# Sliding-window attention and a gated feed-forward block: sums ahead of numerators, masks moved to another engine, and two value steps moved

## The chip, the cores and the metric

The kernel runs on one core of a Trainium2 chip. The metric is the device time of one execution in microseconds (us), as the median of several runs. The engines are PE (TensorE, matmuls), DVE (VectorE), ACT (ScalarE), POOL (GpSimd) and SP, which issues transfers. Each engine works through its own list of instructions in order; semaphores make one wait for another.

## The reference

```python
def _attn_ref(q, k, v):                  # each (8, 8, 576, 64): batch, head, position, width
    scores = scale * np.matmul(q, k.transpose(0, 1, 3, 2))
    rel = pos[:, None] - pos[None, :]
    mask_plain = (rel >= 0) & (rel < 32)
    mask_dil = (rel >= 0) & (rel < 128) & (rel % 4 == 0)
    masks = mask_plain for heads 0 to 3, mask_dil for heads 4 to 7
    scores = np.where(masks, scores, -1e9)
    attn = np.exp(scores - max)
    attn = attn / (sum(attn) + 1e-09)
    return np.matmul(attn, v)

def _moe_ref(x, w_gate, w_val, w_out):   # x: (4608, 512)
    g = x @ w_gate                       # 512 x 1536
    gelu = 0.5 * g * (1.0 + erf(g / sqrt(2)))
    return (gelu * (x @ w_val)) @ w_out  # 1536 x 512
```

The attention's output, with heads side by side, is the x of the second part. Inputs and outputs are fp32; the kernel works in fp16 with fp32 sums.

## The kernel before, in words

**Units.** Attention is done in 32 units n = 0 to 31, each two heads of one batch: batch n // 4, with n % 4 = 0, 1 plain (window of 32) and n % 4 = 2, 3 dilated (every fourth position). A unit goes through four steps, each with its helper:

- Scores: `emit_s` multiplies keys by queries within the band (12 or 10 narrow matmuls, L339 or L369) into four banks of PSUM, and ACT takes the exponential (L349 and L350, or L371) into a tile `P` in SBUF.
- Mask, in one of two ways. With `pe_mask` four matmuls of an identity by a bias tile (L332, L355) put a large negative number into the banks ahead of the scores, and the exponential gives zeros. Without it, `emit_s` hands back a function `emit_mask`, which multiplies `P` by a 0/1 mask on DVE (L379). The set `biased` (L683) names the units that get their mask on PE.
- Values: `emit_pv` multiplies `P` by the values (numerators, "num") and by a tile of ones (sums of weights, "den"), all matmuls at L442. In the narrow form, used in output stages, both lie in three neighbouring banks, V to V+2: the numerators of a plain unit in columns 0 to 575 and its sums in 960 to 1535; those of a dilated unit in 0 to 287 and 512 to 799, and its sums in the rest of the three banks. In the wide form the sums of a dilated unit have two banks of their own.
- Normalisation on DVE: `norm_r` turns the sums over with a 32x32 transpose (dt, L500), takes the reciprocal (rc, L505) and turns it back (rb, L507); `norm_x` multiplies the numerators by it into `xT` (L518 plain, L521 dilated), the x of the feed-forward part.

**Chunks.** The feed-forward part runs over nine chunks c of 512 tokens. Its first half, `ffn1` (L533; `ffn1_two`, L545, for the first two blocks where x comes late), makes 12 blocks of `u_all`, with a GELU on ACT (L557) and a product on DVE (L558) for each. Its second half, here called output stage c, is `ffn2` (L564): four token blocks tb of twelve 512-wide matmuls each, with a copy out of PSUM on ACT (L575) and a store at the end of each.

**Order.** The order of every engine is the order in which the program is written (a manual schedule). Attention units are put between the matmuls of the output stages at places written out by hand: `places` holds for each stage a list such as `1.5s 1.9v`: in token block 1, ahead of matmul 5, the scores of the next unit of `scores[c]`; ahead of matmul 9 the values of the next unit of `values_b[c]`. A 12 means after the block. Output stages 1 and 2 share the list `four`: stage 1 has the scores of units 9, 10 and 11 and the values of 8, 9, 10 and 11 (batch 2), stage 2 the scores of 13, 14, 15 and 16 and the values of 12 to 15 (batch 3). The scores of units 8 and 12 come at the end of the `ffn1` before. A "v" runs the function `pv` of the stage:

```python
def pv(last):
    n = todo.pop(0)
    emit_pv(n, V)
    if not last:
        mask_next()
    norm(n, V)
```

`mask_next` emits the next pending `emit_mask`, if that unit has one. In stages 1 and 2 it stands for the unit whose scores came last. After the stage, `ffn1_two` of the next chunk needs the `xT` of the stage's four units, one for each quarter of its matmuls; the last unit fills the last quarter.

Batches 3 and later are loaded during earlier chunks: loads by SP, casts to fp16 on POOL (L199, L200 for queries and keys, L183, L187 for values).

Of the kernel before, what the change touches and what calls it, by code (L numbers as in the profile page):

```python
# [38 lines left out]
def kernel(  # L39
# [11 lines left out]
    B, H, S, D = q.shape  # L51
    NT, DM = out.shape
    DFF = moe_w_gate.shape[1]
    P = 128
# [11 lines left out]
    PW, PT, DW = 160, 64, 2 * NCL  # L66
    PB = 3 * PW
    PH = PB + P + PT
# [18 lines left out]
    ones = const.tile([P, CH], F16, tag="ones")  # L87
# [165 lines left out]
    def is_plain(n):  # L253
        return n % NHP < NHP // 2
# [125 lines left out]

        return emit_mask

    def emit_pv(n, b0, parts=("num", "den"), wide=False):


        b, hp = n // NHP, n % 2
        vp, vd, vt, vr = tiles["v", b]
        pt = tiles["P", n]
        mms = []

        def add(hl, c0, dims, lhs, p0, pdims, st):

            base = ps[64 * hl : 64 * hl + 64, b0 + c0 // 512, c0 % 512 : c0 % 512 + 1]
            o = bass.AP(tensor=base.tensor, offset=base.offset, ap=[base.ap[0]] + dims)
            rhs = bass.AP(tensor=pt.tensor, offset=pt.offset + p0, ap=[pt.ap[0]] + pdims)
            mms.append((o, lhs, rhs, st))

        def run(n):
            return [[1, n]]

        if is_plain(n):
            if "num" in parts:
                for j in range(5):
                    for hl in range(2):
                        lhs = vp[:, j, hp, 2 * hl, :] if j < 4 else vt[:, hp, 2 * hl, :]
                        w = (PW, PW, PW, P, PT)[j]
                        add(hl, j * P, run(w), lhs, hl * PH + j * PW - (32 if j == 4 else 0), run(w), j in (0, 4))
            if "den" in parts:
                d0 = 1024 if wide else 960

                groups = (
                    ((0, 0, 4, P), (P, P, 3, 32), (PH - PT, 512, 1, PT))
                    if wide
                    else ((0, 0, 1, 64), (64, 64, 1, 64), (PW, P, 3, P), (P, P, 3, 32), (PH - PT, 512, 1, PT))
                )
                for i, (p0, q0, runs, w) in enumerate(groups):
                    for hl in range(2):
                        st = i == 0 or i == (2 if wide else 1)
                        add(hl, d0 + q0, [[P, runs], [1, w]], ones[:, 0:D], hl * PH + p0, [[PW, runs], [1, w]], st)
        else:  # L420
            if "num" in parts:
                for s in range(2):
                    for m in range(3):
                        for hl in range(2):
                            h, p0 = 2 * hp + hl, (2 * s + hl) * DW
                            if m < 2:
                                add(hl, 512 * s + m * NCL, run(P), vd[:, h, 2 * m + s, :], p0 + m * NCL, run(P), m == 0)
                            else:
                                two = [[NCL, 2], [1, 16]]
                                add(hl, 512 * s + P, two, vr[:, h, s, :], p0 + P, two, False)  # L430
            if "den" in parts:

                groups = (
                    ((0, 0, DW, 1024), (1, 0, DW, 1536))
                    if wide
                    else ((0, 0, 192, 288), (0, 192, 96, 800), (1, 0, 96, 896), (1, 96, 192, 1312))
                )
                for i, (s, c, w, c0) in enumerate(groups):
                    for hl in range(2):
                        add(hl, c0, run(w), ones[:, 0:D], (2 * s + hl) * DW + c, run(w), wide or i != 2)  # L440
        for o, lhs, rhs, st in mms:
            nc.tensor.matmul(o, lhs, rhs, start=st, stop=True, skip_group_check=True)  # L442

# [184 lines left out]
    def den(n, b0, wide=False):  # L628
        emit_pv(n, b0, ("den",), wide)
        norm_r(n, b0, wide)  # L630

    def num(n, b0):
        emit_pv(n, b0, ("num",))
        norm_x(n, b0)
# [45 lines left out]
    scores = {0: range(4, 8), 1: range(8, 12), 2: range(12, 17), 3: range(17, 22), 4: range(22, 27), 5: range(27, 32)}  # L680
    values_b = {1: range(8, 12), 2: range(12, 16), 3: range(17, 20), 4: range(22, 24), 5: range(27, 28)}
    values_a = {3: {4: 16}, 4: {2: 20, 6: 21}, 5: {1: 24, 4: 25, 7: 26}, 6: {1: 28, 4: 29, 7: 30, 10: 31}}
    biased = (6, 7, 8, 9, 10, 11, 12, 13, 14, 15)  # L683

    four = "1.5s 1.9v 1.12s 2.6v 2.12s 3.3v 3.12s 3.12v"
    three = "1.4s 1.12v 2.3s 2.12v 3.2s 3.12s 3.12v"
    two = "1.4s 1.12v 2.3s 2.12v 3.2s 3.12s"
    one = "1.4s 1.12v 2.3s 2.12s 3.6s"
# [3 lines left out]
    for c in range(NCH):  # L692
# [11 lines left out]
        for nb in range(NNB):  # L704
            if nb == 0 and c < 2:
                ffn1_two(c, (4, 6) if c == 0 else (6, 0))
            elif nb == 0 and late == "x":
                ffn1_two(c, pairs)
            elif nb > 1 or c > 2 and late != "x":
                ffn1(c, nb, pairs[(nb + swap) % 2])  # L710
            if pend is not None:
                (norm_both_x if is_plain(pend) else norm_x)(pend, SB)
                pend = None
            if nb in pv_at:
                pend = pv_at[nb]
                if is_plain(pend):
                    emit_both(pend, SB)
                    norm_both_r(pend, SB)
                else:
                    emit_pv(pend, SB, wide=True)  # L720
                    norm_r(pend, SB, wide=True)
            if c == 0 and nb in (9, 10):
                t_plain(1, q61, nb - 9, 4 + 2 * (nb - 9), ("act", "dve"))
            if c == 0 and nb in (8, 11):
                rr = rd1.rearrange("p t h r d -> p t (h r d)")
                hp = nb // 11
                t_dil(1, hp, qd1, 4096 + 512 * hp, 5120 + 512 * hp, ("dve", "dve"))
                t_rest(1, hp, (rr[:, 0], rr[:, 1]), 6144 + P * hp)
            if nb == NNB - 1 and c > 0 and s_list:
                n = s_list.pop(0)  # L730
                masks.append(emit_s(n, SB, pe_mask=n in biased))
# [106 lines left out]
```

The softmax here doesn't subtract the row's maximum and nothing guards it: scores larger than these inputs give would overflow.

## Time and profile before

| | |
|---|---|
| median of 7 runs | 362.05 us (360.91 to 363.0) |
| the profiled execution | 362.21 us, of which the span is 360.1 us |
| granted PE clock | 0.991 of full |
| L564, one 512-wide matmul of output stages, x432 | 380 ns from start to end |
| L500 and L507, transposes on DVE | 780 and 778 ns |
| L505, reciprocal | 267 ns |
| L518 and L521, normalised product, plain and dilated | 751 and 1124 ns |
| L371, exponential of a dilated unit | 1129 ns |
| L349 and L350, exponential of a plain unit | 970 and 488 ns |
| L575, copy out on ACT | 597 ns |
| output stage 1, and start of `ffn1_two` behind it | 90.5 to 108.2 us |
| output stage 2, and start of `ffn1_two` behind it | 130.8 to 148.5 us |

One execution was profiled, and all times of single instructions come from it. Matmuls overlap one another, so the time from one start to the next is less than the duration of one. In rows of groups and of the timeline stand the start, the duration, engine, line, operation, the tile written and the tiles read, and in brackets the idle time of the engine before it and whose end it waited for. A row of the waits names the waiting engine and line, the one waited for, the total in us, the number of waits and the longest.

### The profile page before, as it was taken

To read this page: it belongs to the slowest core of one execution; us is meant where nothing else is said; L and a number is where in the kernel's file an instruction comes from. 1 tells how busy PE (TensorE), PEld (TensorE's weight loads), DVE (VectorE), ACT (ScalarE), POOL (GpSimd) and SP (SyncE) were. 2 spreads that over 40 slices of the span, in tenths; PEclk is the share of its full clock that TensorE was granted. 3 is DMA by queue.
4 is the path that set the end of the run, shared out by engine and by line. 5 is a ranking of instruction groups with operands and counts; after the bars stand their busy time and mean duration, and the time that the engine had idled before them with its cause. 6 is when DMAs were issued, how large, how long until landed. Compare 5 with 4: busy or idle time off the path is not lost.

```text
span 360.1 us, 5997 instructions
## 1 busy us (share of the span) xinstructions
PE 344.2 (96%) x2358; PEld 165.7 (46%) x2358; DVE 196.2 (54%) x298; ACT 145.9 (41%) x212; POOL 78.3 (22%) x110
## 2 busy tenths in 40 slices
PE   6789899999989999899999999999999999999995
PEld 2554354444544445444444444544454444444442
DVE  3585446744266325765479838893679613403320
ACT  2633255254542354433653355436543223312321
POOL 2580334540531540054003420050000000000000
PEclk9969999999999999999999999999999999999999
DMA  8999999999899896599438962794100020011002
GB/s 207 233 177 214 215 156 197 191 155 247 185 120 233 185 147 128 140 183 136 102 102 175 156 104 85 170 154 91 60 29 0 19 99 2 1 64 54 0 29 87
DMA packets 107291, 45.30 MB, mean 126 GB/s; under 512 B 83040, under 2 KB 102496, under 8 KB 107264
## 3 DMA queue, kind: packets, MB, share of 16 engines
q1 hardware_dynamic: 84272, 31.21, 38.7%
q0 software_dynamic: 21456, 12.01, 27.5%
q10 hardware_dynamic: 1536, 1.70, 2.0%
q8 instruction: 18, 0.29, 0.4%
q14 instruction: 9, 0.07, 0.1%
HBM read 40.13 MB, written 9.44 MB: 138 GB/s over the span
## 4 chain that ended last, share of the span: by engine, by line
PE 82%; DMA 10%; DVE 4%; POOL 1%; ACT 1%; issue 0%; SPq 0%; POOLq 0%; ACTq 0%
PE ps L533 44%; PE ps L564 26%; DMA qd<-in_k_dram 5%; PE ps L442 4%; DMA xT<-in_q_dram 3%; PE ps L545 3%; DMA vr<-in_v_dram 2%; PE ps L339 1%; DVE xT L521 1%; PE ps L369 1%; PE ps L455 1%; DVE dt L500 1%; DVE rb L507 1%; PE ps L355 1%; PE ps L332 1%; DVE P L379 0%
## 5 line engine op out<-in xcount | busy, mean ns | idle before, releaser
L557 ACT ACTIVATE g<-ps 128x512 f16<-128x512 f32 x108 | 63.6, 597 | 124.3 <-PE ps L533 110.9
L558 DVE SCALAR_TENSOR_TENSOR u_all<-g,ps 128x512 f16<-128x512 f16 x108 | 72.6, 683 | 75.4 <-PE ps L533 66.2
L564 PE MATMUL ps<-wo,u_all 128*128 128x512 f16 x432 | 101.0, 380 | 0.4 <-ACT osb L575 0.3
L533 PE MATMUL ps<-xT,wg 128*128 128x512 f16 x392 | 100.7, 379 | 0.2
L533 PE MATMUL ps<-xT,wv 128*128 128x512 f16 x392 | 100.6, 379 | 0.0
L564 PEld LDWEIGHTS <-u_all 128*128 128x128 f16 x432 | 39.2, 98 | 44.6 <-issue 0.5
L533 PEld LDWEIGHTS <-wv 128*128 128x128 f16 x392 | 38.3, 98 | 46.5 <-issue 0.2
L533 PEld LDWEIGHTS <-wg 128*128 128x128 f16 x392 | 37.2, 98 | 44.7 <-issue 2.0
L575 ACT ACTIVATE osb<-ps 128x512 f32<-128x512 f32 x33 | 19.7, 597 | 48.4 <-PE ps L564 48.4
L500 DVE STREAM_TRANSPOSE dt<-ps 128x576 f32<-128x576 f32 x25 | 19.5, 780 | 25.2 <-PE ps L442 25.1
L199 POOL CAST qp<-st 128x2048 f16<-128x2048 f32 x6 | 11.4, 1893 | 100.6 <-DMA st<-in_k_dram 51.1
L507 DVE STREAM_TRANSPOSE rb<-rc 128x576 f32<-128x576 f32 x32 | 24.9, 778 | 1.1
L371 ACT ACTIVATE P<-ps 128x1152 f16<-128x1152 f32 x16 | 18.1, 1129 | 12.7 <-PE ps L369 12.7
L349 ACT ACTIVATE P<-ps 128x960 f16<-128x960 f32 x16 | 15.5, 970 | 9.4 <-PE ps L339 9.3
L521 DVE TENSOR_TENSOR xT<-ps,rb 128x576 f16<-128x576 f32 x16 | 17.8, 1124 | 0.3
L577 DVE TENSOR_SCALAR osb<-ps 128x512 f32<-128x512 f32 x3 | 2.1, 692 | 27.8 <-PE ps L564 27.8
L545 PE MATMUL ps<-xT,wg 128*128 128x512 f16 x40 | 15.4, 385 | 1.4 <-DVE xT L521 0.9
L545 PE MATMUL ps<-xT,wv 128*128 128x512 f16 x40 | 15.2, 380 | 0.0
L442 PE MATMUL ps<-P,ones 128*64 128x192 f16 (+5 forms) x174 | 11.6, 248 | 1.6 <-DVE P L379 0.7
L379 DVE TENSOR_TENSOR P<-P,mask_p 128x1344 f16<-128x1344 f16 x10 | 9.2, 926 | 6.8 <-ACT P L350 6.8
L379 DVE TENSOR_TENSOR P<-P,mask_d 128x1152 f16<-128x1152 f16 x8 | 6.1, 757 | 11.1 <-ACT P L371 11.1
L470 DVE STREAM_TRANSPOSE dt<-ps 64x576 f32<-64x576 f32 x14 | 10.9, 780 | 0.4
(83 smaller groups left out, 268.0 us busy)
## 6 DMA issues: line engine op xcount, KB each, us to landing
out_dram<-osb SPq DMA_DIRECT2D x36, 256.0 KB, 2.0
sv<-in_v_dram SPq DMA_DIRECT2D x40, 128.0 KB, 3.7
st<-in_q_dram SPq DMA_DIRECT2D x24, 128.0 KB, 3.5
st<-in_k_dram SPq DMA_DIRECT2D x24, 128.0 KB, 2.9
qd<-in_q_dram POOLq DMA_DIRECT2D x7, 256.0 KB, 4.9
qd<-in_k_dram POOLq DMA_DIRECT2D x7, 256.0 KB, 6.9
vd<-in_v_dram POOLq DMA_DIRECT2D x7, 256.0 KB, 6.9
wg<-in_moe_w_gate_dram POOLq DMA_DIRECT2D x3, 512.0 KB, 8.2
```

The costliest lines, as they stand in the source:

```text
L349: nc.scalar.activation(pt[:, :, 0:PB], sb[:, 0, :, 0:PB], AF.Exp, bias=0.0, scale=scale)
L371: nc.scalar.activation(pt, ps[:, b0 : b0 + 4, 0:DW], AF.Exp, bias=0.0, scale=scale)
L442: nc.tensor.matmul(o, lhs, rhs, start=st, stop=True, skip_group_check=True)
L500: nc.vector.transpose(dst, den)
L507: nc.vector.transpose(rb.rearrange("p (b c) -> p b c", c=32), bass.AP(tensor=rc.tensor, offset=rc.offset, ap=[rc.ap[0], [1, 18], [0, 32]]),)
L521: nc.vector.tensor_tensor(dst.rearrange("p (i m s) -> p i m s", m=2, s=2), num, rb.rearrange("p (s m i) -> p i m s", s=2, m=2), ALU.mult,)
L533: nc.tensor.matmul(ps[:, b0 + gi, :], w[:, kc, ns], xT[kc][:, tok], start=(kc == 0), stop=(kc == NKC - 1))
L545: nc.tensor.matmul(ps[:, pairs[nb] + gi, :], w[:, kc, ns], xT[kc][:, tok], start=(kc == 0), stop=(kc == NKC - 1),)
L557: nc.scalar.activation(g, ps[:, b0, :], AF.Gelu)
L558: nc.vector.scalar_tensor_tensor(u_all[:, nb, :], g, USCALE, ps[:, b0 + 1, :], ALU.mult, ALU.mult)
L564: nc.tensor.matmul(ps[:, bank, :], u_all[:, fc, tb * P : (tb + 1) * P], wo_t[fc // 4][:, fc % 4, :], start=(fc == 0), stop=(fc == NNB - 1),)
L575: nc.scalar.activation(osb, ps[:, bank, :], AF.Copy, bias=0.0, scale=1.0 / USCALE)
```

## The change

Three edits. `emit_pv` emits the sums of weights before the numerators, in both forms. The units 9, 10, 11, 13, 14 and 15 leave the set `biased`, so that their masks are multiplied on DVE; 6, 7, 8 and 12 stay. In the list `four`, the first values go from 1.9 to 1.6 and the second from 2.6 to 2.4.

```diff
-    def emit_pv(n, b0, parts=("num", "den"), wide=False):
+    def emit_pv(n, b0, parts=("den", "num"), wide=False):
...
         if is_plain(n):
-            if "num" in parts:
-                for j in range(5):
-                    ...
             if "den" in parts:
                 d0 = 1024 if wide else 960
...
                         add(hl, d0 + q0, [[P, runs], [1, w]], ones[:, 0:D], hl * PH + p0, [[PW, runs], [1, w]], st)
+            if "num" in parts:
+                for j in range(5):
+                    ...
         else:
+            if "den" in parts:
+                groups = (...)
+                ...
             if "num" in parts:
                 for s in range(2):
...
-            if "den" in parts:
-                groups = (...)
-                ...
         for o, lhs, rhs, st in mms:
             nc.tensor.matmul(o, lhs, rhs, start=st, stop=True, skip_group_check=True)
...
-    biased = (6, 7, 8, 9, 10, 11, 12, 13, 14, 15)
+    biased = (6, 7, 8, 12)
 
-    four = "1.5s 1.9v 1.12s 2.6v 2.12s 3.3v 3.12s 3.12v"
+    four = "1.5s 1.6v 1.12s 2.4v 2.12s 3.3v 3.12s 3.12v"
```

The loops that move (shown as `...`) are the same before and after.

More of the change, by code (lines that the diff above doesn't have):

```diff
@@ L401, in emit_pv @@
         if is_plain(n):
-            if "num" in parts:
-                for j in range(5):
[L404 to L407, printed above, removed]
             if "den" in parts:
@@ L419, in emit_pv @@
                         add(hl, d0 + q0, [[P, runs], [1, w]], ones[:, 0:D], hl * PH + p0, [[PW, runs], [1, w]], st)
-        else:
+            if "num" in parts:
+                for j in range(5):
+                    for hl in range(2):
+                        lhs = vp[:, j, hp, 2 * hl, :] if j < 4 else vt[:, hp, 2 * hl, :]
+                        w = (PW, PW, PW, P, PT)[j]
+                        add(hl, j * P, run(w), lhs, hl * PH + j * PW - (32 if j == 4 else 0), run(w), j in (0, 4))
+        else:
+            if "den" in parts:
+                groups = (
+                    ((0, 0, DW, 1024), (1, 0, DW, 1536))
+                    if wide
+                    else ((0, 0, 192, 288), (0, 192, 96, 800), (1, 0, 96, 896), (1, 96, 192, 1312))
+                )
+                for i, (s, c, w, c0) in enumerate(groups):
+                    for hl in range(2):
+                        add(hl, c0, run(w), ones[:, 0:D], (2 * s + hl) * DW + c, run(w), wide or i != 2)
             if "num" in parts:
@@ L430, in emit_pv @@
                                 add(hl, 512 * s + P, two, vr[:, h, s, :], p0 + P, two, False)
-            if "den" in parts:
[L433 to L440, printed above, removed]
         for o, lhs, rhs, st in mms:
```

## The prediction

> **What bounds the kernel now.** I read the page first, then the waits of PE, then the chain of waits through output stages 1 and 2, then the timeline of DVE, ACT and POOL around them. A unit is a pair of heads (32 units, four to a batch). "pv" of a unit is its 20 matmuls of L442: numerators, and sums of weights against ones.
>
> ```profile
> PE 344.2 (96%) x2358; PEld 165.7 (46%) x2358; DVE 196.2 (54%) x298; ACT 145.9 (41%) x212; POOL 78.3 (22%) x110
> ```
>
> PE is busy for 96% of the span, so whatever PE no longer does looks like a gain, and DVE at 54% looks free. But these are averages. The waits of PE show where it isn't the bound:
>
> ```profile
> PE ps L442 <- DVE xT L521: 1.8, 2, 1.1
> ...
> PE ps L545 <- DVE xT L521: 0.9, 2, 0.5
> ```
>
> Four waits, 2.7 us, and all four are at the end of output stages 1 and 2, the two stages that the change edits. There PE waits for DVE's normalisation (L521). The chain of waits through stage 2:
>
> ```profile
> 134.66 0.57 PE ps L332 x4
> ...
> 138.06 0.49 PE ps L355 x4
> ...
> 142.44 0.49 PE ps L355 x4
> 142.93 0.37 PE ps L369 x12
> 143.30 0.75 PE ps L564 x3
> 144.06 0.68 PE ps L442 x20
> 144.75 0.80 DVE dt L500
> 145.57 0.28 DVE rc L505
> 145.88 0.79 DVE rb L507
> 146.69 1.14 DVE xT L521
> 147.83 0.04 issue
> 147.87 0.74 PE ps L442 x16
> 148.64 0.80 DVE dt L500
> ```
>
> L332 and L355 are bias masks on PE: they are what is removed. From 144.75 on the chain is DVE: the normalisation of unit 14 (dt, rc, rb, xT: 3.07 us), pv of unit 15, its normalisation, and only then the last quarter of L545, at 151.75. So the stage ends at a fixed distance, 7.0 us, behind the start of dt for its third unit, if DVE does nothing else in between. Stage 1 is alike: dt of unit 10 at 104.44, L545 freed at 111.42. **What counts is when that third dt starts**; the sum below is made on it.
>
> **Part 1, the bias masks.** Units 9, 10, 11 (stage 1) and 13, 14, 15 (stage 2) lose four matmuls each: by the rows 0.57 us for 9 and 13, 0.49 for the other four, 3.10 us of PE in all. In their place each gets a multiply of its weights on DVE (L379). The prices:
>
> ```profile
> 54.44 0.86 DVE L379 TENSOR_TENSOR P<-P,mask_p 128x1344 f16<-128x1344 f16 x1 [2.43 <-ACT P L350]
> 58.55 1.57 DVE L379 TENSOR_TENSOR P<-P,mask_p 128x1344 f16<-128x1344 f16 x1
> 176.35 0.76 DVE L379 TENSOR_TENSOR P<-P,mask_d 128x1152 f16<-128x1152 f16 x1 [2.21 <-ACT P L371]
> ```
>
> 0.86 plain, 0.76 dilated. The 1.57 lay over two POOL casts (58.37 to 60.37). The place matters more than the price: `pv` emits a unit's matmuls, then the multiply of the next unit, then the normalisation. So dt now queues on DVE behind a multiply that waits for ACT's exponential of the next unit. Behind dt stand the rest of the normalisation and, through it, the next pv on PE, which needs the banks.
>
> **Part 2, values sooner.** The first pv goes from behind nine matmuls of the second token block to behind six, one matmul after the scores of the next unit; the second from behind six matmuls of the third block to behind four. The second to third scores thus move behind 8 matmuls after the second pv instead of 6. Values loads are no issue: those of batch 2 were cast by 72.6, used at 96.2; those of batch 3 by 99.6, used at 136.5. No DMA is moved.
>
> **Part 3, sums ahead of numerators.** The matmuls are the same and so I cost PE at nothing. A gain would need dt to start before the numerators end. In the narrow form used in output stages, sums and numerators share banks (plain: bank V+1; dilated: V and V+1). In the trace one row shows how such a case waits: two groups of transposes go to the first bank, columns 0 to 127 and 128 to 255, and the second waited for the copy of the first, which ended at 16.75.
>
> ```profile
> 16.80 0.66 PE L312 MATMUL ps<-ident,xT 16*128 16x16 f32 x8 [0.95 <-DVE qTd L315]
> ```
>
> So a wait goes by bank and not by column. dt then waits for the last numerator, just as it waited for the last sum: 0 us. Only the wide dilated form keeps them in separate banks (units 26, 30, 31); dt comes some 0.3 us sooner there, in stages where PE waits for nothing: 0 us as well.
> The Trainium skill, "PSUM — Partial Sum Buffer", section "PSUM bank collisions raise a hardware error", says to guard by bank, not by address, which speaks against this part in the same way; by that rule the sum is the one below, by columns it would be the first rival's.
>
> **The sum, stage 2.** A 512-wide matmul takes 0.216 us (17 from 130.81 to 134.49), a turn to narrow ones 0.10. Scores of 13 start at 134.49 + 0.10 = 134.59. From scores to the end of the exponential a plain unit took 1.85 us (54.84 to 56.69): 136.44. Multiply: +0.03 + 0.86 = 137.33. dt of unit 12 at 137.36; before it was 137.35. So the normalisation of 12 ends where it did (2.79 us: 140.15), and pv 13 starts at 140.20 against 140.26. PE is there long before: scores 0.40, one matmul 0.32, pv 0.72, six 1.40, scores 0.37, four 0.96 make 138.76. It waits 1.4 us, a new wait that eats the bias time saved on 13 and 14.
> Then pv 13 to 140.91; eight matmuls to 142.64; ACT stores the block 0.20 behind (142.84 to 143.44; before it began at 142.48), and only then does the exponential of 15: 143.44 + 1.13 = 144.57 (its scores, at 142.74, would have allowed 143.22). Multiply +0.03 + 0.76 = 145.36. dt of 14 at 145.39 instead of 144.75: **+0.64 us**. With the old places, 6 matmuls instead of 8 there, it would be 0.43 less.
> **Stage 1** is the same to a few hundredths, but POOL casts until 96.28 and the multiply of 9 would be ready at 96.16. By the 1.57 row, where the multiply ended 0.7 after the first cast did, it waits: +0.12. dt of 8 is at 97.17 (97.10 before), dt of 10 at 105.15 (104.44): **+0.71 us**. Bounds of this meeting: nothing, or the whole of the two casts that run there, 2.45 us, if the data they wait for land 2.4 us later.
> The Trainium skill, "SBUF — State Buffer", section "Who interferes with whom", has such a multiply, of two SBUF inputs, block wholly against a POOL read that came first; that would make the same +0.12.
>
> Behind the third dt nothing changes, so the sum is **+1.35 us**: 362.21 of the profiled run (span 360.1 and 2.1 around it) to 363.6, and on the median of 362.05, 363.4. The saved 3.10 us of PE shows up as PE's idle time. A difference under 0.3% (1.1 us) is about what can't be told from none.
>
> **The rivals.**
> Faster: dt waits by columns. Then the sums of 13 are done while its numerators wait for unit 12; after that wait only 0.30 us of PE remain instead of 0.71, so dt of 14 comes at 140.50 + 1.73 + 0.20 + 0.60 + 1.13 + 0.03 + 0.76 + 0.03 = 144.98, late by 0.23, but dt of 15 follows the product of 14 at once instead of 0.82 later (147.82 to 148.64). Net -0.57 a stage, -1.1 to -1.35 for both as the turns fall: 360.8. Against it stands the row at 16.80. For it: no row shows DVE reading a bank beside PE's writing.
> About the same: the multiply of the third unit is ready sooner, if ACT does the exponential of 15 ahead of the store or PE's wait before pv 13 is shorter than 1.4. With the multiply fully hidden, dt of 14 follows pv 14, at 144.65: -0.1 a stage, 361.85. Against it: ACT's order is the program's, and the store comes first.
> Slower by more: the multiply of 9 in stage 1 meets the 1.89 us cast of L199. That cast waits for a load, from 80.2 to 93.83; should it start later than 94.4, it holds the multiply for what is left of it, and the whole chain of stage 1 moves with it: up to 1.9 to 2.4 us, 365.3 to 365.8.
>
> **How the numbers follow.** My sum 0.70 (in four fifths of it over 1.1 us: 0.56 slower, 0.14 same), waits by column 0.10 (faster), multiply hidden 0.10 (0.08 same, 0.02 faster), meeting the cast 0.10 (slower). That makes faster 0.12, same 0.22, slower 0.66. My sum's own terms (1.85 of the exponential, 0.10 of a turn, the meeting on POOL) reach from about 362.4 to 364.8. The range goes from 361.2 (leaving out the first rival) to 365.0 (leaving out most of the last).
>
> **What would show it.** Right: L442 waits for L518 in both stages, some 1.4 us each, and for L521 some 1.9 and 1.5 us (1.1 and 0.7 before); dt of the third unit ends its idle time with the multiply of L379 just before it; L545 is freed 0.6 to 0.7 later from the stage's start. Wrong: dt of L500 beginning within the numerators of its own unit in these stages; no wait of L442 at the second pv; or PE's idle time growing by less than 3 us, which would mean that a part of the bias time came through as a gain.

## The result and the profile after

The changed kernel takes 363.69 us (median of 13 runs, 362.66 to 364.56), the kernel before 362.06 us (32 runs): a ratio of 1.0047, 95% interval 1.0036 to 1.0058, or 1.6 us slower. The forecast was 363.4. The profiled execution took 363.28 us with a span of 361.2, against 362.21 and 360.1.

First the page of the changed kernel, the busy time of each engine:

```profile
PE 341.7 (95%) x2334; PEld 165.6 (46%) x2334; DVE 200.4 (55%) x304; ACT 145.4 (40%) x212; POOL 78.1 (22%) x110
```

PE does 2.5 us less than before (344.2), in a span 1.1 us longer: its idle time grew from 15.9 to 19.5 us. On balance all of that lies in stages 1 and 2: from the first L564 of the stage to the last quarter of L545 PE is idle for 6.3 us in the two together, against 2.7 before. Where it went stands in the waits of PE (total, number, longest):

```profile
PE ps L442 <- DVE xT L521: 2.2, 2, 1.3
...
PE ps L442 <- DVE xT L518: 1.9, 2, 1.1
PE ps L564 <- ACT osb L575: 1.6, 5, 0.3
...
PE ps L545 <- DVE xT L521: 1.0, 2, 0.5
...
PE ps L442 <- DVE xT L480: 0.3, 1, 0.3
```

New are the waits for L518, one in each of the stages 1 and 2 at the second pv (1.06 and 0.85 us), and the one for L480, which lies in chunk 5 and not in these stages at all. L564's waits for the copy of L575 rise from 0.3 us to 1.6: the four new ones, 0.31 us each, lie in the two stages too. They don't add to the stage's length, since two of them come ahead of PE's longer wait for L518 in the same stage and the other two while the chain below runs through ACT and DVE. The chain of waits through stage 2 has turned from PE to DVE and ACT:

```profile
136.33 0.49 ACT P L350
136.82 0.02 issue
136.84 0.86 DVE P L379
137.70 0.70 DVE dt L500
...
139.61 0.77 DVE xT L518
140.38 0.04 issue
140.42 0.78 PE ps L442 x20
141.21 1.85 PE ps L564 x8
143.05 0.02 issue
143.08 0.40 ACT osb L575
143.48 0.09 issue
143.57 1.13 ACT P L371
144.70 0.02 issue
144.73 0.76 DVE P L379
145.49 0.70 DVE dt L500
...
152.40 0.81 PE ps L545 x3
```

The reader sees the sum of the prediction link by link: exponential, multiply (L379), normalisation, the second pv, eight matmuls, the store's copy, the exponential of unit 15, its multiply, and the third dt. (In this view a piece begins where the one before it ends; by the timeline, which the table below uses, that dt starts at 145.40.) The distance from the start of the stage's first token block to the third dt is the number to watch, because from there to the last quarter of L545 both kernels need 7.0 us:

| third dt, us after the stage's start | stage 1 | stage 2 |
|---|---|---|
| before | 104.44 - 90.50 = 13.94 | 144.75 - 130.81 = 13.94 |
| changed | 104.81 - 90.39 = 14.42 | 145.40 - 131.18 = 14.22 |

That is +0.48 and +0.28 us. A third piece lies behind the stages: from the wait of L545 for L349 in chunk 4 to the end of the span the kernel before takes 360.1 - 186.38 = 173.72 us, the changed one 361.2 - 187.03 = 174.17, +0.45. The three make 1.21 us; the start-up was 0.11 shorter in this run. It differs from run to run: up to the start of stage 1 all kernels of this document run the same program, and in their ten profiled runs that point lies between 89.82 and 91.61 us.

### The profile page after: what moved, and what is told of

Same layout as the page of the kernel before. It is cut to its first block, busy times and chain, and to the rows that moved or that the text cites. A ratio compares the mean times of both kernels' runs of the same rounds, so it can differ in the third digit from the quotient of the medians.

```text
span 361.2 us, 5953 instructions
## 1 busy us (share of the span) xinstructions
PE 341.7 (95%) x2334; PEld 165.6 (46%) x2334; DVE 200.4 (55%) x304; ACT 145.4 (40%) x212; POOL 78.1 (22%) x110
## 4 chain that ended last, share of the span: by engine, by line
PE 78%; DVE 11%; ACT 4%; DMA 3%; issue 2%; ACTq 0%; DVEq 0%
PE ps L533 42%; PE ps L564 24%; PE ps L545 4%; DMA xT<-in_k_dram 3%; PE ps L442 3%; DVE rb L507 2%; DVE dt L500 2%; PE ps L339 1%; DVE P L379 1%; DVE dt L470 1%; DVE xT L521 1%; ACT P L371 1%; ACT osb L575 1%; PE ps L369 1%; DVE u_all L558 1%
## 5 line engine op out<-in xcount | busy, mean ns | idle before, releaser
L558 DVE SCALAR_TENSOR_TENSOR u_all<-g,ps 128x512 f16<-128x512 f16 x108 | 72.6, 683 | 76.2 <-PE ps L533 65.1
L564 PE MATMUL ps<-wo,u_all 128*128 128x512 f16 x432 | 100.9, 380 | 1.7 <-ACT osb L575 1.6
L533 PE MATMUL ps<-xT,wg 128*128 128x512 f16 x392 | 100.7, 379 | 0.2
L533 PE MATMUL ps<-xT,wv 128*128 128x512 f16 x392 | 100.6, 379 | 0.0
L564 PEld LDWEIGHTS <-u_all 128*128 128x128 f16 x432 | 39.7, 98 | 45.8 <-issue 1.7
L533 PEld LDWEIGHTS <-wv 128*128 128x128 f16 x392 | 38.3, 98 | 46.4 <-issue 0.3
L533 PEld LDWEIGHTS <-wg 128*128 128x128 f16 x392 | 37.3, 98 | 44.1 <-issue 1.4
L575 ACT ACTIVATE osb<-ps 128x512 f32<-128x512 f32 x33 | 19.7, 597 | 51.5 <-PE ps L564 51.5
L379 DVE TENSOR_TENSOR P<-P,mask_p 128x1344 f16<-128x1344 f16 x12 | 10.9, 915 | 18.4 <-ACT P L350 18.4
L349 ACT ACTIVATE P<-ps 128x960 f16<-128x960 f32 x16 | 15.5, 970 | 8.3 <-PE ps L339 8.2
L521 DVE TENSOR_TENSOR xT<-ps,rb 128x576 f16<-128x576 f32 x16 | 17.8, 1125 | 0.3
L442 PE MATMUL ps<-P,ones 128*64 128x192 f16 (+5 forms) x174 | 11.9, 251 | 6.3 <-DVE xT L521 2.2
L545 PE MATMUL ps<-xT,wg 128*128 128x512 f16 x40 | 15.8, 396 | 1.5 <-DVE xT L521 1.0
L379 DVE TENSOR_TENSOR P<-P,mask_d 128x1152 f16<-128x1152 f16 x12 | 9.1, 756 | 12.3 <-ACT P L371 12.3
L545 PE MATMUL ps<-xT,wv 128*128 128x512 f16 x40 | 15.7, 392 | 0.0
L442 PEld LDWEIGHTS <-ones 128*64 128x64 f16 x174 | 7.3, 111 | 14.7 <-issue 13.4
```

Source lines behind the costliest of these rows:

```text
L379: nc.vector.tensor_tensor(pt, pt, mb, ALU.mult)
L521: nc.vector.tensor_tensor(dst.rearrange("p (i m s) -> p i m s", m=2, s=2), num, rb.rearrange("p (s m i) -> p i m s", s=2, m=2), ALU.mult,)
L533: nc.tensor.matmul(ps[:, b0 + gi, :], w[:, kc, ns], xT[kc][:, tok], start=(kc == 0), stop=(kc == NKC - 1))
L545: nc.tensor.matmul(ps[:, pairs[nb] + gi, :], w[:, kc, ns], xT[kc][:, tok], start=(kc == 0), stop=(kc == NKC - 1),)
L558: nc.vector.scalar_tensor_tensor(u_all[:, nb, :], g, USCALE, ps[:, b0 + 1, :], ALU.mult, ALU.mult)
L564: nc.tensor.matmul(ps[:, bank, :], u_all[:, fc, tb * P : (tb + 1) * P], wo_t[fc // 4][:, fc % 4, :], start=(fc == 0), stop=(fc == NNB - 1),)
```

## The experiments

**The masks alone** (places and order as before).

```diff
-    biased = (6, 7, 8, 9, 10, 11, 12, 13, 14, 15)
+    biased = (6, 7, 8, 12)
```

> The kernel before with one edit: units 9, 10, 11, 13, 14 and 15 leave `biased`; places and the order of sums and numerators stay. Theory (the third dt sets the stage's end, and the masks cost only through the place of the third scores): the second pv waits for unit 8's product some 0.9 us, the third scores come two matmuls sooner than in the changed kernel, and dt of unit 10 (14) starts about 13.8 us after the start of the stage's first token block, against 13.94 before and 14.42 (14.22) changed: 361.8 us, 0.1 to 0.4 under the kernel before. Rival (the multiplies on DVE are the whole cost of stages 1 and 2, wherever the values stand): dt at 14.2 to 14.4, 362.8 us.

Measured: 362.3 us, ratio 0.9995 (0.9982 to 1.0009), so the times show no difference. In the trace the third dt comes 13.77 and 13.79 us after the stage's start, as the theory had it to 0.03 us, and L442 waits for L518 0.4 us in each stage (0.9 expected). Six masks on DVE in place of PE don't lengthen the stages by themselves; by the trace they shorten each by some 0.15 us. But 3.1 us of bias matmuls bring no more than that.

**The places alone.**

```diff
-    four = "1.5s 1.9v 1.12s 2.6v 2.12s 3.3v 3.12s 3.12v"
+    four = "1.5s 1.6v 1.12s 2.4v 2.12s 3.3v 3.12s 3.12v"
```

> The kernel before with one edit: places 1.6v and 2.4v instead of 1.9v and 2.6v; masks and order stay. Theory: with the bias on PE no multiply stands ahead of dt, and the third pv comes after the same matmuls in all, so dt of unit 10 starts at 13.9 to 14.0 us from the stage's start as before: 362.06 us, within 0.2. Rival (the move by itself is the cost, since the second pv comes before the first product is done): a wait of L442 for L518 of 0.3 us or more in each stage, 362.5 to 362.8 us.

Measured: 362.04 us, ratio 0.9990 (0.9979 to 1.0000). The third dt comes at 13.94 and 13.94, as before to the hundredth, and no wait for L518 appears. So neither of these two edits costs anything alone; the 0.48 and 0.28 us need both together.

**The order alone.**

```diff
-    def emit_pv(n, b0, parts=("num", "den"), wide=False):
+    def emit_pv(n, b0, parts=("den", "num"), wide=False):
...
     (sums emitted ahead of numerators, as in the change)
```

> The kernel before with one edit: sums of weights ahead of numerators, in the narrow and the wide form. Theory (waits go by bank): nothing in stages 1 and 2; but in the wide form the sums now need first the two banks that DVE's product of the plain unit before (L480) reads last, which showed as a new wait of PE of 0.3 us in chunk 5 and some 0.2 us in chunk 6 of the changed kernel: 362.5 us. Rival 1 (prediction: the order costs nothing anywhere): 362.06. Rival 2 (dt waits by columns): 360.8.

Measured: 362.55 us, ratio 1.0003 (0.9985 to 1.0021): the times can't tell 0 from 0.45, though they exclude a gain of 1.1 us. The trace tells more. In stages 1 and 2 the third dt stands at 13.93 and 13.93. Its timeline around pv of unit 10 (start, duration, engine, line):

```profile
103.89 0.44 PE L442 MATMUL ps<-P,ones 128*64 128x192 f16 x8
104.17 0.28 PE L442 MATMUL ps<-P,vd 128*64 128x128 f16 x4
...
104.42 0.18 PE L442 MATMUL ps<-P,vr 128*64 128x32 f16 x2
104.54 0.82 PE L564 MATMUL ps<-wo,u_all 128*128 128x512 f16 x3
104.65 0.78 DVE L500 STREAM_TRANSPOSE dt<-ps 128x576 f32<-128x576 f32 x1 [0.97 <-PE ps L442]
```

The sums are done at 104.33, DVE has been idle for 0.97 us, and dt still starts at 104.65, after the last numerators (104.60), 0.76 us after pv began (before: 0.77). The wait doesn't go by column. In chunk 5 the wide form, whose sums have banks of their own, meets the other side of this. First the kernel before, then this one:

```profile
237.13 1.53 DVE L480 TENSOR_TENSOR xT<-ps,rb 64x576 f16<-64x576 f32 x2
...
238.33 0.30 PE L442 MATMUL ps<-P,vd 128*64 128x128 f16 x4
```

```profile
237.35 1.51 DVE L480 TENSOR_TENSOR xT<-ps,rb 64x576 f16<-64x576 f32 x2
...
238.92 0.44 PE L442 MATMUL ps<-P,ones 128*64 128x288 f16 x4 [0.29 <-DVE xT L480]
```

The two products of the plain unit before read first one pair of banks, then the other. Numerators went into the first pair; sums go into the second, which comes free 0.75 us later. In the kernel before, pv of this unit began at 238.33 without a wait, while DVE was reading the second pair until 238.66: matmuls wait for the banks that they write, and not for the whole of both products. Unit 30 in chunk 6 is alike: its pv starts 1.17 us behind the start of the four L533 ahead of it, 0.96 in the kernel before. Nor does dt of the three wide units come sooner for having its sums first, since products of L558 stand ahead of it on DVE. From L545's wait in chunk 4 to the end this kernel takes 360.7 - 186.61 = 174.09 us, 0.37 more than before.

**The wide form's order undone** in the changed kernel.

```diff
+        if wide and len(parts) == 2:
+            mms = mms[4:] + mms[:4]
         for o, lhs, rhs, st in mms:
```

> The changed kernel with one part undone: in the wide form numerators come first again. Theory: the new wait for L480 in chunk 5 goes, and 0.45 us of the difference with it: 363.25 us. Rival (the wide order costs nothing): 363.7.

Measured: 363.15 us, ratio 1.0021 (1.0007 to 1.0036). The wait for L480 (L482 in this kernel, which is two lines longer) is gone, and the last stretch takes 360.7 - 187.02 = 173.68, as before. All runs of this document agree on that stretch: 173.66 to 173.75 us in the six kernels with numerators first in the wide form, 174.09 to 174.17 in the four with sums first. So the order of the wide form costs some 0.4 us by the traces; the medians (363.15 against 363.69, from different sessions) go the same way. Stage 2 stands as in the changed kernel (14.22). In stage 1 this run took longer (14.98): the multiply of unit 9 ran for 1.64 us instead of 0.86.

**The third unit's mask back on PE**, in the changed kernel.

```diff
-    biased = (6, 7, 8, 12)
+    biased = (6, 7, 8, 11, 12, 15)
```

> The changed kernel with one part undone: the masks of units 11 and 15 go back to PE, so that no multiply stands ahead of the third dt. Theory (what is late is the place of the third scores, two matmuls later behind the second pv that waited): PE's four bias matmuls put the third pv where the multiply had put dt, which starts at 104.77 instead of 104.81: 363.6 us, 0.1 under the changed kernel. Rival (the multiply of the third unit by itself, 0.76 us ahead of dt, is the cost): dt 0.4 to 0.5 us sooner in each stage, 362.8 us.

Measured: 363.71 us, ratio 1.0042 (1.0027 to 1.0056), the changed kernel's time. The third dt comes at 14.14 and 14.15: 0.07 sooner in stage 2, and 0.28 in stage 1, where 0.21 of it is the multiply of unit 9, which took 1.07 us in the changed kernel and 0.86 here. Without the multiply ahead of it, dt waits for PE instead (1.41 us in each stage). So taking away the 0.76 us of the third multiply doesn't bring the stage back.

**The second place undone**, in the changed kernel.

```diff
-    four = "1.5s 1.6v 1.12s 2.4v 2.12s 3.3v 3.12s 3.12v"
+    four = "1.5s 1.6v 1.12s 2.6v 2.12s 3.3v 3.12s 3.12v"
```

> The changed kernel with one part undone: the second values go back from 2.4 to 2.6; the masks stay on DVE and the first values at 1.6. Theory: the second pv starts when unit 8's product is done, wherever it stands; with two matmuls fewer behind it the third scores, their exponential and their multiply come 0.43 us sooner, and so does the third dt (14.0 and 13.8 us from the stage's start): 0.86 us less, 362.8 us. Rival (the first place, 1.6, is what turned the masks into a cost): 363.7 us.

Measured: 362.79 us, ratio 1.0017 (1.0007 to 1.0026). The third dt comes at 13.77 and 13.79, as with the masks alone (stage 1 0.2 sooner than expected, since the multiply of unit 9 didn't meet the cast). In stage 2, which starts at 131.59 in this run:

```profile
144.70 0.76 DVE L379 TENSOR_TENSOR P<-P,mask_d 128x1152 f16<-128x1152 f16 x1 [0.36 <-ACT P L371]
145.38 0.78 DVE L500 STREAM_TRANSPOSE dt<-ps 128x576 f32<-128x576 f32 x1
```

So 1.6v is harmless, and 2.4v with the masks on DVE is the cost of the two stages, up to the 0.21 us of the meeting on POOL: the second pv can't start before unit 8's product, and what is put behind it, eight matmuls instead of six, delays the third scores, in stage 2 by 14.22 - 13.79 = 0.43 us, two matmuls of 0.216. By the trace, this kernel differs from the one before by -0.17 and -0.15 us in the stages and by +0.4 behind them, 0.1 in all; the medians differ by 0.6 (0.3 to 0.9). The rest of some 0.5 us isn't explained.

**Values earlier, masks on PE**, since the third dt sets the end.

```diff
-    four = "1.5s 1.9v 1.12s 2.6v 2.12s 3.3v 3.12s 3.12v"
+    four = "1.4v 1.5s 1.12v 2.0s 2.9v 2.10s 3.6v 3.12s"
```

> The kernel before with one edit: the list of stages 1 and 2 is 1.4v 1.5s 1.12v 2.0s 2.9v 2.10s 3.6v 3.12s, so that each normalisation of DVE starts as soon as the one before allows; all masks of these stages stay on PE, the order is as before. Theory (the stage ends 7 us behind the third dt, until PE's own work is longer): the third dt comes some 11.6 us from the stage's start instead of 13.9, PE's matmuls are then the longer path (about 19.4 us from the stage's start to the last quarter of L545 against 20.9), 1.5 us less in each stage: 359.1 us. Rival (the stage is bound by PE, and DVE's waits at its end are only the rest): 361 to 362 us. Rival 2 (the first values, two matmuls sooner, wait for a bank that ACT still copies out): over 362 us.

Measured: 363.55 us, ratio 1.0039 (1.0027 to 1.0051), slower: the expectation failed on the time. The third dt came at 101.74 - 89.99 = 11.75 as expected, and two other waits took the gain:

```profile
PE ps L564 <- ACT osb L575: 2.7, 3, 1.2
...
PE ps L545 <- ACT P L349: 1.6, 2, 1.1
```

The timeline shows the first: the exponential of unit 11 stands in ACT's order ahead of the copy that frees the bank of the next token block.

```profile
102.92 1.13 ACT L371 ACTIVATE P<-ps 128x1152 f16<-128x1152 f32 x1 [2.76 <-PE ps L369]
...
103.95 0.59 ACT L575 ACTIVATE osb<-ps 128x512 f32<-128x512 f32 x1
104.59 1.46 PE L564 MATMUL ps<-wo,u_all 128*128 128x512 f16 x6 [1.17 <-ACT osb L575]
```

The second is the exponential of unit 16, put last, holding the banks that L545 needs in chunk 3 (1.15 us). So the time is what rival 2 had, but not by its wait: the first values started without one. And the third dt no longer says when the stage ends: the last quarter of L545 starts 20.54 and 22.38 us after the stage's start, against 20.92 and 20.94 before.

**The same with those two waits taken away**: third scores behind the copy, unit 16 sooner.

```diff
-    four = "1.5s 1.9v 1.12s 2.6v 2.12s 3.3v 3.12s 3.12v"
+    four = "1.4v 1.5s 1.12v 2.0s 2.9v 2.12s 3.6s 3.8v"
```

> The kernel before with the list 1.4v 1.5s 1.12v 2.0s 2.9v 2.12s 3.6s 3.8v: values early as in e5_early, but the third scores behind the store of the third block, so that their exponential doesn't hold up the copy that frees the block's bank, and the fourth scores (unit 16, stage 2 only) five matmuls before the end, so that their exponential is done when L545 wants its banks. Theory (those two waits of 1.17 and 1.15 us are all that ate the gain of e5_early): no wait of L564 over 0.4 us and none of L545 for L349 in chunk 3; the stages are some 1.1 us shorter each than before, 360.0 us. Rival (with the third scores two matmuls later the third unit's exponential, or DVE, takes the place of these waits): 361.5 us or more.

Measured: 359.48 us against 362.25 of the kernel before in the same session, ratio 0.9918 (0.9903 to 0.9934), 0.8% faster than the kernel before and, by the medians of different sessions, 1.2% faster than the changed one. No wait of PE is left in the two stages. The third dt comes at 103.36 - 91.61 = 11.75 and 141.94 - 130.21 = 11.73, and the last quarter of L545 starts 19.21 and 19.69 us after the stage's start, against 20.92 and 20.94. The theory had 1.1 us a stage; it is 1.7 and 1.25. On the page, PE's busy line:

```profile
PE 342.4 (96%) x2358; PEld 164.6 (46%) x2358; DVE 196.1 (55%) x298; ACT 146.2 (41%) x212; POOL 78.3 (22%) x110
```

PE has its 2358 matmuls again, bias masks included; its idle time is 358.2 - 342.4 = 15.8 us. That is no less than the 15.9 before, though the 2.7 us in the two stages are gone: in this run PE was idle for 10.8 us ahead of stage 1, in the profiled run of the kernel before for 8.2.

## Why the prediction was right, point by point

**What counts is the third dt**: right, and the step on which the rest stands. In the kernel before, the changed one and the six runs that move single parts of the change, the last quarter of L545 starts 6.98 to 7.01 us behind it. With values earlier that ends: first other waits, then PE's own work set the end.

**The bias time doesn't come through**: right. Less PE work in stages 1 and 2 turned into PE's idle time, +3.6 us where "less than 3" would have refuted it. The waits forecast for it were too long: 1.4 us each for L518 and 1.9 and 1.5 for L521, against 1.06 and 0.85, and 1.28 and 0.89. At the second pv of stage 2, PE came 0.44 us later than summed, 0.31 of it the wait for the copy, which the sum left out, and pv itself started 0.15 sooner.

**Where the time goes in the stages**: the mechanism was right (second pv pinned by unit 8's product, third scores behind eight matmuls, copy, exponential, multiply), the size was not: +0.64 forecast and +0.28 measured in stage 2, +0.71 and +0.48 in stage 1. The term that was mis-sized is the handover between two instructions of the same engine. I had put dt 0.03 us behind the end of the multiply, and the exponential at the end of the copy. The timeline of the changed kernel:

```profile
136.84 0.86 DVE L379 TENSOR_TENSOR P<-P,mask_p 128x1344 f16<-128x1344 f16 x1 [5.77 <-ACT P L350]
137.62 0.78 DVE L500 STREAM_TRANSPOSE dt<-ps 128x576 f32<-128x576 f32 x1
...
143.08 0.60 ACT L575 ACTIVATE osb<-ps 128x512 f32<-128x512 f32 x1 [3.56 <-PE ps L564]
...
143.57 1.12 ACT L371 ACTIVATE P<-ps 128x1152 f16<-128x1152 f32 x1
...
144.73 0.76 DVE L379 TENSOR_TENSOR P<-P,mask_d 128x1152 f16<-128x1152 f16 x1 [0.80 <-ACT P L371]
...
145.40 0.78 DVE L500 STREAM_TRANSPOSE dt<-ps 128x576 f32<-128x576 f32 x1
```

dt starts at 137.62, 0.08 before the multiply's 0.86 us are over; the exponential 0.11 before the copy ends; the last dt 0.09 before its multiply ends. Three handovers, each 0.11 to 0.12 shorter than I had them, make 0.34 of the 0.36 us. (An instruction that does need the one before it on its engine, as rc does dt, still starts 0.03 behind its end.) The profile before had shown it: the second exponential of a plain unit started at 56.21, while the first, from 55.34 for 0.97 us, ran to 56.31.

**The meeting with POOL in stage 1**: +0.12 forecast, and 1.07 - 0.86 = 0.21 measured in the changed kernel, where the cast of L200 ran until 96.41 and the multiply had started at 96.05; 0.00 in three runs with unit 9's mask on DVE whose multiply began after the cast (masks alone, third mask back, second place back: 0.86 us each).

```profile
95.80 0.61 POOL L200 CAST qp<-st 64x512 f16<-64x512 f32 x1
...
96.05 1.07 DVE L379 TENSOR_TENSOR P<-P,mask_p 128x1344 f16<-128x1344 f16 x1 [5.77 <-ACT P L350]
```

The multiply ended 0.71 us behind the cast, just as in the 1.57 row. Read like that, the row gives nothing for the meeting that the prediction had summed (96.28 + 0.71 is before 96.16 + 0.86), and not the 0.12 that it named: that was the whole multiply put behind the cast. The meeting was longer than summed because the cast ended 0.24 us later in the stage than in the kernel before. The Trainium skill, "SBUF — State Buffer", section "Who interferes with whom", has a later starter blocked wholly, which would end it at 96.41 + 0.86 = 97.27; it ended at 97.12, so these rows agree but for 0.15 us.

**The order at nothing**: right for the narrow form (13.93 with the order alone, and dt behind the last numerator), which fits what the Trainium skill, "PSUM — Partial Sum Buffer", section "PSUM bank collisions raise a hardware error", asks for: to guard by bank. Wrong for the wide form. The failed step is "in stages where PE waits for nothing: 0 us as well". PE waited for nothing there because the numerators went to the pair of banks that came free first; I looked at who waits for the sums and not at what the sums, now first, wait for. It cost 0.45 us in the changed kernel's profiled run. The 0.3 us by which dt was to come sooner there didn't show either.

So +1.35 became 0.76 in the stages and 0.45 behind them, 1.21, and 1.6 by the medians (1.3 to 2.1). That the forecast of 363.4 came so close is in part luck: two errors of opposite sign, and a rest that it knew nothing of. What makes up the last 0.4 us was not settled: the profiled run of the changed kernel lies 0.4 under its median, and stage 1 varies with the length of the multiply by up to 0.56 us (14.98 with the wide order undone, 14.42 in the changed kernel). One profiled run of each kernel can't say how often that happens.

**Rivals.** Waits by column: refuted by the order alone. A hidden third multiply: refuted by the trace of the changed kernel, in which DVE is idle for 0.80 us ahead of that multiply and dt stands right behind it. The meeting on POOL: it exists, at 0.21 us in the changed kernel's profiled run and 0.78 us at most in the others (where no cast is recorded beside it), not at 2.

## What to carry to other kernels

A matmul taken off a 96% busy PE is worth next to nothing in a stage whose end is set by a chain on another engine (here some 0.15 us of 1.55 a stage); find the one event from which the stage's end is at a fixed distance, and move that. When two edits each cost nothing, their sum need not: with the masks on DVE, PE reached the second pv early and had to wait there, and only then did it matter how many matmuls stand behind that pv. And when the order of two groups is swapped, ask what the group that is now first waits for, besides who waits for it.

## What the runs showed of the hardware that had not been expected

In these traces an instruction of DVE or ACT starts some 0.1 us before the recorded end of the one before it on the same engine, if it doesn't read its result (137.62 against 137.70, 143.57 against 143.68).

A multiply of L379 took 1.64 us instead of 0.86 in the run with the wide order undone, though the casts on POOL had ended at 94.89 and it ran from 95.47:

```profile
94.84 0.77 POOL L213 DMA_DIRECT2D vd<-in_v_dram  x1
...
95.47 1.64 DVE L379 TENSOR_TENSOR P<-P,mask_p 128x1344 f16<-128x1344 f16 x1 [5.76 <-ACT P L350]
95.59 1.24 POOL L218 DMA_DIRECT2D vr<-in_v_dram  x2
...
96.81 1.19 POOL L183 CAST vp<-sv 128x1024 f16<-128x1024 f32 x1
```

Until 96.81 POOL only issued transfers, by its record. In three other runs the same multiply ran beside L213 at 0.86 us, and with the masks alone beside the first issue of L218 too (multiply from 96.47, issue from 96.72 for 0.63 us). So neither holds it by itself. Whether the second issue did, or whether POOL's recorded spans, which are rough, start the cast too late, stays open.
